# A gated MLP block: fifteen of sixteen token tiles transposed by DMA as f16 parts, in place of f32 transposes on TensorE

## The chip, the cores and the metric

The kernel runs on one core of one Trainium2 chip, in one launch. The metric is the device time of that launch in microseconds (us), which is better when it is lower. Times of a kernel are given as the median of several executions; one more execution is recorded by the hardware profiler, and its rows are what this document quotes. TensorE is the matrix engine, VectorE, ScalarE and POOL are the vector engines, and SP only issues DMAs. In the rows they are called PE (PEld is TensorE's loading of weights), DVE, ACT, POOL and SP (SPq is the queue of DMAs that SP issues).

## The reference

One block works on 2048 tokens of width 576. A state space convolution comes first; its output x goes through a layer norm with learned scale and shift (from the condition c), then through a gated MLP whose gate mixes tokens:

```python
h = _layernorm(x, axis=-1) * (1 + cb) + sb
z = _gelu(jnp.einsum("bsd,df->bsf", h, w_in))        # 576 -> 4608
z1 = z[..., :Fh]                                     # Fh = 2304
z2 = _layernorm(z[..., Fh:], axis=-1)
g = jnp.einsum("ts,bsf->btf", w_sp, z2) + b_sp[None, :, None]
x = x + gb * jnp.einsum("bsf,fd->bsd", z1 * g, w_out)
```

The products are wanted to nearly f32 accuracy. The kernel gets this from f16 matmuls: each f32 operand is split into a high part hi = f16(v) and a low part lo = f16(v - hi), and hi·hi, hi·lo and lo·hi are added up in PSUM.

## The kernel before

The program has three stages. The convolution runs to about 443 us. Then phase_a, the z2 stage, makes h and the second half of z for all tokens, and prepares operands for later. From about 693 us phase_b makes z1, the token mixing g and the output; it takes more than half of the time, and the change does not touch it.

phase_a works on 16 token tiles of 128 rows. For tile b, x1_load(b) reads the 128x576 rows; ln2_stats(b), roots and ln2_rows(b) make the normalised rows n (tile n2, f32, 128x640: the last 64 columns are there twice, through a tensor_copy) on VectorE. turn(b) transposes n on TensorE in five 128x128 pieces against an identity, into the PSUM tile pt. turn_hi(b) on ScalarE and turn_lo(b) on VectorE read pt and write the f16 parts into nt: nine slabs of 128 tokens, four of high parts, four of low parts, and a ninth that has the last 64 columns as high parts on partitions 0 to 63 and as low parts on 64 to 127. turn_lo also stores nt to DRAM (n2_d) through POOL's queue, for phase_b.

z2_mm(b, h) multiplies nt with the weights wz for column block h: five blocks, four of 512 columns and one of 256, 14 matmuls each, so 70 a tile. z2_gelu(b, h) takes each block out of PSUM (six banks, tile pz) through gelu into z, on ScalarE. There are two z buffers. z2_stats collects statistics on VectorE (bsz), roots(b) turns them into scale and shift (nm), z2_diff and z2_norm normalise z in place, and z2_store(b) writes it to DRAM (z2_d) through POOL's queue in two DMAs.

All of phase_a goes through an object that keeps every engine's instructions in the order in which the program calls them, SP's DMAs as well. In the main loop (line 1243) the iteration of tile b holds, in this order: DMAs due (LD); z2_mm(b,0); due squares (A0); gelu (b,0); statistics and roots of tile b-1 and of the rows of tile b+2; z2_norm(b-1); ln2_rows(b+2); x1_load(b+4); z2_mm(b,1); turn(b+1); gelu (b,1); z2_store(b-1); z2_stats of the first columns; turn_hi(b+1); turn_lo(b+1); z2_mm(b,2); gelu (b,2); further due work (A1); z2_mm(b,3), gelu, more statistics; ln2_stats(b+3); due work (V1); z2_mm(b,4), gelu.

The due work belongs to later stages. side_load, side_sum, side_hi and side_lo split the first half of w_in (tiles wst, wso). wsp_load and out_load read pieces of w_sp and w_out (tile wsst, two buffers, two pieces a tile) in A1 of one iteration, and norm_sp and norm_out square and sum them on ScalarE in A0 of the next, ahead of its gelu (b,0). block_load, wsp_sums, wsp_hi and wsp_lo (tile xz) prepare w_sp from tile 8 on.

The first iteration is special, since the weights wz are still being made there. For the blocks q = 3 and 4, start_sum(q) squares the raw weights on ScalarE (its junk output goes to wz), win_scale(5 + q) forms a total over partitions on TensorE (two small matmuls pz<-acc,ones) and a power-of-two scale on VectorE, start_hi(q) writes the high parts on ScalarE and start_lo(q) the low parts on VectorE. They stand in iteration 0: start_sum(3) and win_scale(8) ahead of gelu (0,0), start_hi(3) and start_lo(3) behind it, then roots, ln2_rows(2), z2_mm(0,1), gelu (0,1), start_sum(4), win_scale(9), start_hi(4) and start_lo(4). Ahead of the loop (line 1230) tile 0 is transposed and the rows of tile 1 are made.

Of the kernel before, what the change touches and what calls it, by code (L numbers as in the profile page):

```python
# [9 lines left out]
F32 = mybir.dt.float32  # L10
F16 = mybir.dt.float16
BF = mybir.dt.bfloat16
I32 = mybir.dt.int32
AF = mybir.ActivationFunctionType
ALU = mybir.AluOpType
# [3 lines left out]
D = 576  # L19
# [742 lines left out]
class Mlp:  # L762
# [342 lines left out]
    def ln2_rows(self, b):  # L1105

        V = self.nc.vector
        x, m, r = self.xts.pop(b), self.mvx.pop(b)[:, 0, 0:1], self.rx.pop(b)
        n = self.ns[b] = self.ap.tile([128, 640], F32, name="n2")
        V.scalar_tensor_tensor(n[:, :D], x, m, self.mrow[:, 1], op0=ALU.subtract, op1=ALU.mult)  # L1110
        V.scalar_tensor_tensor(n[:, :D], n[:, :D], r, self.mrow[:, 0], op0=ALU.mult, op1=ALU.add)
        V.tensor_copy(n[:, D:], n[:, 512:D])

    def turn(self, b):

# [53 lines left out]
            self.nc.gpsimd.dma_start(self.z2_d[:, b // 4, :, 2 * (b % 2) + h, b % 4 // 2].rearrange("f p c -> p f c"), z[:, h])  # L1169

    def phase_a(self):
        self.prods, self.z1s, self.n2, self.bsp, self.gbs, self.wfs = {}, {}, {}, {}, {}, {}
        ap = self.ap = self.pool(self.c2, "ap", 2)
        cpa = ExitStack()
        self.pa = self.pool(cpa, "pa", 6, space=PSUM)
        self.ps1 = lambda: self.pa.tile([128, 512], F32, name="pz")
        self.zp = self.pool(self.c2, "zp", 2)
        self.wp = self.pool(self.ctx, "wp", 7, side="right")

        self.fp = self.pool(self.ctx, "fp", 1, side="right")  # L1180
        self.wso = ap.tile([128, 4, 10, 128], F16, name="wso", bufs=1)
        self.nc, plain = self.tied, self.nc
        self.nc.vector.memset(self.wso[64:, :, 9], 0.0)

        LD, PE, A0, A1, V0, V1 = range(6)
        sides = [[[] for _ in range(6)] for _ in range(17)]

        def side(b, k, fn, *a):
            sides[b][k].append((fn, a))

        def do(b, k):
            for fn, a in sides[b][k]:
                fn(*a)

        for q in range(5):
            side(2 * q, LD, self.side_load, q)
            side(2 * q + 1, A0, self.side_sum, q)
            side(2 * q + 1, PE, self.win_scale, q)
            side(2 * q + 1, A1, self.side_hi, q)
            side(2 * q + 1, V1, self.side_last, q)  # L1200
            side(2 * q + 1, V1, self.side_lo, q, 0)
            side(2 * q + 2, V0, self.side_lo, q, 1)
        for h in range(2):
            side(1, LD, self.bsp_load, ap, h)
            side(2, A0, self.norm_bsp, h)
        for i in range(8):
            side(2 + i // 2, A1, self.wsp_load, 0, i, ap)
            side(3 + i // 2, A0, self.norm_sp, 0, i)
        for i in range(12):
            side(6 + i // 2, A1, self.out_load, ap, i)  # L1210
            side(7 + i // 2, A0, self.norm_out, i)
        for i in range(6):
            side(12 + i // 2, A1, self.wsp_load, 1, i, ap)
            side(13 + i // 2, A0, self.norm_sp, 1, i)
        side(13, V1, self.sums_out)
        side(14, PE, self.scales_out)
        side(6, V1, self.sums_sp, 0)
        side(7, PE, self.scales_sp, 0)
        side(11, PE, self.scales_gate, 0)
        for i in range(7):  # L1220
            side(9 + i, V0, self.wsp_sums, i)
            side(9 + i, A1, self.wsp_hi, 0, i)
            side(9 + i, V1, self.wsp_lo, 0, i)
            side(8 + i, V1, self.block_load, 0, i)
        side(13, LD, self.z1_rows, 0)
        side(13, LD, self.bias_load, 0)
        for f in (0, 9, 1):
            side(13, LD, self.z1_load, 0, f)

        for b in range(2):  # L1230
            if b == 1:
                self.ln2_stats(1)
                self.roots(x=1)
                self.ln2_rows(1)
            if b == 0:
                self.turn(0)
                self.turn_hi(0)
                self.start_lo(2)
                self.start_load(4)
                self.x1_load(4)  # L1240
                self.turn_lo(0)
        self.ln2_stats(2)
        for b in range(16):
            do(b, LD)
            self.z2_mm(b, 0)
            do(b, A0)
            if b == 0:
                self.start_sum(3)
                self.win_scale(8)
            self.z2_gelu(b, 0)  # L1250
            if b == 0:
                self.start_hi(3)
                self.start_lo(3)
            if b > 0:
                self.z2_stats(b - 1, 5)
            self.roots(b - 1 if b > 0 else None, b + 2 if b + 2 < 16 else None)
            if b > 0:
                if b % 2:
                    self.z2_diff(b - 1)
                self.z2_norm(b - 1)  # L1260
            if b + 2 < 16:
                self.ln2_rows(b + 2)
            if 4 < b + 4 < 16:
                self.x1_load(b + 4)
            do(b, PE)
            self.z2_mm(b, 1)
            if b + 1 < 16:
                self.turn(b + 1)
            self.z2_gelu(b, 1)
            if b > 0:  # L1270
                self.z2_store(b - 1)
            if b == 0:
                self.start_sum(4)
                self.win_scale(9)
                self.start_hi(4)
            do(b, V0)
            self.z2_stats(b, 0, 1)
            if b + 1 < 16:
                self.turn_hi(b + 1)
            if b == 0:  # L1280
                self.start_lo(4)
            if b + 1 < 16:
                self.turn_lo(b + 1)
            self.z2_mm(b, 2)
            self.z2_gelu(b, 2)
            do(b, A1)
            self.z2_mm(b, 3)
            self.z2_stats(b, 2, 3)
            self.z2_gelu(b, 3)
            if b + 3 < 16:  # L1290
                self.ln2_stats(b + 3)
            do(b, V1)
            self.z2_stats(b, 4)
            self.z2_mm(b, 4)
            self.z2_gelu(b, 4)
        cpa.close()
        self.z2_stats(15, 5)
        self.roots(15)
        self.z2_norm(15)
        self.z2_store(15)  # L1300
        self.nc = plain
        self.c2.close()
# [315 lines left out]
```

## Time and profile before

| | us |
|---|---|
| median of 3 executions (1796.09 to 1799.17) | 1798.02 |
| the profiled execution | 1798.62 |
| its span, first to last instruction | 1796.9 |
| TensorE busy, whole span | 1695.7 |
| VectorE busy | 1128.8 |
| ScalarE busy | 785.6 |
| z2 stage, from the first transposes to the last z2 product | about 250 |

The page of the profile gives totals over the whole span. Other views cut it: busy time by stage, the timeline (every instruction with its start, its duration and, in brackets, the idle time before it and what ended it), the groups of instructions of one shape, the list of waits, and the DMA issues with the time from issue to landing. Nearly all work of phase_a goes through one helper line (L132), so its rows are told apart by the tiles that they write and read: pt<-ident,n is a transpose on TensorE, pz<-wz,nt a z2 product, z<-pz,sc a gelu, z<-z,nm,r a normalisation, wsst<-wsst a square for a norm.

### The profile page before, as it was taken

What the parts mean: (1) busy time and instruction counts of PE and PEld (TensorE: products, weight loads), DVE (VectorE), ACT (ScalarE), POOL (GpSimd) and SP (SyncE); (2) the same over time, 40 slices, a digit from 0 to 9 for tenths busy, and PEclk for the clock granted to TensorE, in tenths of its full rate; (3) what the DMA queues carried; (4) which work ended last, traced back from release to release, by engine and by line L of the source; (5) the groups of instructions that cost most, each with busy time, mean ns of one, the idle gap of its engine ahead of it and who ended that gap; (6) DMA issues with size and microseconds to landing.
All of it is one profiled execution on the core that took longest, in us unless ns stands there. A gap on an engine that the chain in (4) does not pass through costs nothing.

```text
span 1796.9 us, 34078 instructions
## 1 busy us (share of the span) xinstructions
PE 1695.7 (94%) x14202; PEld 1197.6 (67%) x14202; DVE 1128.8 (63%) x2253; ACT 785.6 (44%) x1021; POOL 224.0 (12%) x350
## 2 busy tenths in 40 slices
PE   4687999996899999999999999999999999999999
PEld 1344555565455545877787777877778777887787
DVE  6987999857888997999784444474222265222322
ACT  4658999844476666555441322241111132011110
POOL 1321232342122211000000000000000000000000
PEclk8788999998899999999999999999999999999999
DMA  8457445779588788877564675562655472555520
GB/s 274 139 196 243 139 119 163 195 207 314 169 266 261 241 259 246 301 277 257 206 216 148 240 250 206 212 250 92 227 192 197 173 264 69 176 181 175 199 83 27
DMA packets 153034, 361.57 MB, mean 201 GB/s; under 512 B 24832, under 2 KB 68224, under 8 KB 150960
## 3 DMA queue, kind: packets, MB, share of 16 engines
q1 hardware_dynamic: 110272, 167.30, 29.4%
q0 software_dynamic: 33120, 153.95, 25.8%
q10 hardware_dynamic: 9488, 38.16, 5.3%
q8 instruction: 111, 1.82, 0.4%
q14 instruction: 43, 0.35, 0.1%
HBM read 256.86 MB, written 93.05 MB: 195 GB/s over the span
## 4 chain that ended last, share of the span: by engine, by line
PE 51%; DVE 16%; DMA 7%; issue 4%; ACT 4%; SPq 0%; POOL 0%; ACTq 0%; DVEq 0%; POOLq 0%
PE ps L1324 9%; PE ps L1359 8%; PE ps L1361 8%; PE ps L1360 8%; PE pz L132 3%; PE ps L1408 3%; PE ps L1409 3%; PE ps L1410 3%; DMA raw<-in_w_spT 2%; DVE zset L1066 2%; DVE gt L1373 2%; DMA z_d<-z 2%; ACT z L132 1%; DVE bsz L132 1%; PE pk L132 1%
## 5 line engine op out<-in xcount | busy, mean ns | idle before, releaser
L1359 PE MATMUL ps<-wsp,zset 128*128 128x256 f16 x2016 | 549.5, 273 | 2.8 <-DVE gt L1373 2.6
L1361 PE MATMUL ps<-wsp,zset 128*128 128x256 f16 x2016 | 549.5, 273 | 0.2 <-DVE zset L1066 0.2
L1360 PE MATMUL ps<-wsp,zset 128*128 128x256 f16 x2016 | 549.5, 273 | 0.0
L132 PE MATMUL pz<-wz,nt 128*128 128x512 f16 (+1 forms) x1120 | 227.2, 363 | 9.0 <-ACT nt L132 5.5
L1373 DVE SCALAR_TENSOR_TENSOR gt<-ps,sc,bsp 128x512 f32<-128x512 f32 x36 | 27.0, 749 | 316.1 <-PE ps L1361 316.1
L1324 PE MATMUL ps<-n2q,wf 128*128 128x512 f16 x1008 | 223.3, 379 | 0.6 <-DMA wf<-win_d 0.6
L1359 PEld LDWEIGHTS <-zset 128*128 128x128 f16 x2016 | 197.5, 98 | 29.7 <-DVE gt L1373 3.2
L1360 PEld LDWEIGHTS <-zset 128*128 128x128 f16 x2016 | 197.2, 98 | 26.1
L1361 PEld LDWEIGHTS <-zset 128*128 128x128 f16 x2016 | 197.3, 98 | 23.3 <-DVE zset L1066 0.5
L132 PEld LDWEIGHTS <-nt 128*128 128x128 f16 x1120 | 110.2, 100 | 117.4 <-ACT nt L132 7.2
L1324 PEld LDWEIGHTS <-wf 128*128 128x128 f16 x1008 | 98.6, 98 | 112.6 <-DMA wf<-win_d 1.1
L1336 POOL DMA_DIRECT2D zset<-set_d x96 | 51.1, 532 | 969.3 <-PE ps L1361 939.3
L1329 ACT ACTIVATE z<-ps,sc 128x512 f32<-128x512 f32 x56 | 37.8, 681 | 280.5 <-PE ps L1324 278.0
L1409 PE MATMUL ps<-wout,z 128*128 128x288 f16 x448 | 128.1, 286 | 0.0
L1408 PE MATMUL ps<-wout,z 128*128 128x288 f16 x448 | 128.1, 286 | 0.0
L1410 PE MATMUL ps<-wout,z 128*128 128x288 f16 x448 | 128.1, 286 | 0.0
L1373 DVE SCALAR_TENSOR_TENSOR gt<-ps,sc,gt 128x512 f32<-128x512 f32 (+1 forms) x180 | 121.9, 694 | 5.8 <-DVE gt L1373 0.5
L1066 DVE TENSOR_TENSOR zset<-raw,zset 128x1024 f16<-128x1024 f32 x48 | 58.6, 1220 | 74.7 <-ACT zset L1065 74.7
L1065 ACT ACTIVATE zset<-raw 128x1024 f16<-128x1024 f32 x48 | 50.3, 1051 | 97.5 <-PE ps L1361 70.1
L132 ACT ACTIVATE z<-pz,sc 128x512 f32<-128x512 f32 (+1 forms) x80 | 49.6, 646 | 56.8 <-DMA z_d<-z 44.4
L1418 DVE TENSOR_TENSOR ot<-ot,ps 128x288 f32<-128x288 f32 x32 | 14.2, 452 | 82.7 <-ACT ot L1417 82.7
L369 PE MATMUL ps<-ln_x,r1t 128*128 128x288 f32 x128 | 43.6, 499 | 19.0 <-issue 12.6
(311 smaller groups left out, 2827.5 us busy)
## 6 DMA issues: line engine op xcount, KB each, us to landing
zset<-set_d POOLq DMA_DIRECT2D x96, 896.0 KB, 4.9
set_d<-zset ACTq DMA_DIRECT2D x36, 896.0 KB, 5.8
raw<-z_d SPq DMA_DIRECT2D x48, 512.0 KB, 4.6
wf<-win_d SPq DMA_DIRECT2D x72, 320.0 KB, 3.4
raw<-in_w_spT SPq DMA_DIRECT2D x43, 512.0 KB, 6.0
z_d<-z POOLq DMA_DIRECT2D x32, 576.0 KB, 7.8
u_d<-st1o POOLq DMA_DIRECT2D x16, 576.0 KB, 4.5
u<-u_d SPq DMA_DIRECT2D x36, 256.0 KB, 4.8
```

What stands on the lines that cost most here:

```text
L132: return self.tc.keep_in_program_order(f(*a, **k))
L1065: nc.scalar.activation(o[:, k, 0], t, AF.Copy)
L1066: nc.vector.tensor_tensor(o[:, k, 1], t, o[:, k, 0], op=ALU.subtract)
L1324: nc.tensor.matmul(pm.rearrange("p (t c) -> p t c", t=4), w[:, kw], self.n2[q][:, :, kn], start=i == 0, stop=i == len(Z1) - 1)
L1336: self.nc.gpsimd.dma_start(o, self.set_d[n // 4, n % 4])
L1359: T.matmul(pm, z[:, a, 0, c], w[:, b, 0], start=i + half == 0, stop=False, skip_group_check=True)
L1360: T.matmul(pm, z[:, a, 0, c], w[:, b, 1], start=False, stop=False, skip_group_check=True)
L1361: T.matmul(pm, z[:, a, 1, c], w[:, b, 0], start=False, stop=i == 7, skip_group_check=True)
L1373: V.scalar_tensor_tensor(dst, pm, inv, to, op0=ALU.mult, op1=ALU.add)
L1408: T.matmul(pl, p[:, 1, ts], w[:, 0, hs], start=st, stop=sp)
L1409: T.matmul(pa, p[:, 0, ts], w[:, 0, hs], start=st, stop=False)
L1410: T.matmul(pa, p[:, 0, ts], w[:, 1, hs], start=False, stop=sp)
```

## The change

For tiles 1 to 15 the rows are split as they lie, tokens on partitions, and the f16 result is transposed by a DMA on SP's queue. Tile 0 keeps turn, turn_hi and turn_lo. Four new functions stand for the three:

```diff
-        n = self.ns[b] = self.ap.tile([128, 640], F32, name="n2")
+        n = self.ns[b] = self.ap.tile([128, 640], F32, name="n2", bufs=1)
...
-        V.tensor_copy(n[:, D:], n[:, 512:D])
+        if b == 0:
+            V.tensor_copy(n[:, D:], n[:, 512:D])
+
+    def rows_hi(self, b):
+        A, n = self.nc.scalar, self.ns[b]
+        o = self.nrs[b] = self.ap.tile([128, 9, 128], F16, name="nr", bufs=1)
+        A.activation(o[:, 0:4], n[:, :512].rearrange("p (k c) -> p k c", k=4), AF.Copy)
+        A.activation(o[:, 8, :64], n[:, 512:D], AF.Copy)
+
+    def rows_lo(self, b):
+        V, n, o = self.nc.vector, self.ns.pop(b), self.nrs[b]
+        V.tensor_tensor(o[:, 4:8], n[:, :512].rearrange("p (k c) -> p k c", k=4), o[:, 0:4], op=ALU.subtract)
+        V.tensor_tensor(o[:, 8, 64:], n[:, 512:D], o[:, 8, :64], op=ALU.subtract)
+
+    def rows_turn(self, b):
+        nt = self.nts[b] = self.ap.tile([128, 9, 128], F16, name="nt", bufs=3)
+        self.nc.sync.dma_start_transpose(nt, self.nrs.pop(b).rearrange("p k c -> p (k c)"))
+
+    def rows_store(self, b):
+        self.nc.gpsimd.dma_start(self.n2_d[b // 4, :, b % 4], self.nts[b])
```

Their places in phase_a: tile 1 is split and transposed ahead of the loop, and iteration b splits and transposes tile b+2, one tile earlier than turn did, while it stores the nt of tile b+1.

```diff
@@ ahead of the loop, b == 1
                 self.ln2_rows(1)
+                self.rows_hi(1)
+                self.rows_lo(1)
+                self.rows_turn(1)
@@ in the loop
             self.z2_mm(b, 1)
-            if b + 1 < 16:
-                self.turn(b + 1)
+            if b + 2 < 16:
+                self.rows_hi(b + 2)
             self.z2_gelu(b, 1)
...
             self.z2_stats(b, 0, 1)
-            if b + 1 < 16:
-                self.turn_hi(b + 1)
             if b == 0:
                 self.start_lo(4)
+            if b + 2 < 16:
+                self.rows_lo(b + 2)
+                self.rows_turn(b + 2)
             if b + 1 < 16:
-                self.turn_lo(b + 1)
+                self.rows_store(b + 1)
             self.z2_mm(b, 2)
```

n2 has one buffer instead of two, and nr, the split rows, has one.

More of the change, by code (lines that the diff above doesn't have):

```diff
@@ L1171, in phase_a @@
     def phase_a(self):
+        self.nrs = {}
         self.prods, self.z1s, self.n2, self.bsp, self.gbs, self.wfs = {}, {}, {}, {}, {}, {}
```

## The prediction

> **What bounds the kernel now.** First I read the busy time by stage, cut at the borders of the z2 loop (first transposes 443 us, last z2 product 693 us).
>
> ```profile
> core 0: us, PE busy (x) PEld busy (x) DVE busy (x) ACT busy (x) POOL busy (x), PEclk, DMA share, GB/s
> 444.00:474.00 30.00, 22.43 (x93) 10.56 (x93) 26.49 (x79) 13.28 (x16) 3.36 (x5) 0.83 0.59 188
> 507.00:693.00 186.00, 178.87 (x947) 92.93 (x946) 162.99 (x497) 121.40 (x181) 39.18 (x51) 1.00 0.82 255
> ```
>
> Two regimes. From 507 us on TensorE is 96% busy, VectorE 88%, the DMA engines 82%: TensorE leads, the others close behind. In the first 30 us TensorE is a quarter idle at a granted clock of 0.83, and VectorE (26.5 of 30 us) leads. Next the timeline of one steady tile, TensorE:
>
> ```profile
> 565.31 0.71 PE L132 MATMUL pt<-ident,n 128*128 128x128 f32 x5
> 565.86 13.78 PE L132 MATMUL pz<-wz,nt 128*128 128x512 f16 x70
> 579.48 0.71 PE L132 MATMUL pt<-ident,n 128*128 128x128 f32 x5
> ```
>
> Five transposes take 565.86 - 565.31 = 0.55 us, and the 70 products of a tile 579.48 - 565.86 = 13.62 us. So all that TensorE can save is 15 x 0.55 = 8.3 us. The timeline of ScalarE gives what a tile really takes, from the first gelu of tile 3 to that of tile 15:
>
> ```profile
> 507.27 0.69 ACT L132 ACTIVATE z<-pz,sc 128x512 f32<-128x512 f32 x1 [2.32 <-DMA z_d<-z]
> 689.33 0.69 ACT L132 ACTIVATE z<-pz,sc 128x512 f32<-128x512 f32 x1 [4.55 <-DMA z_d<-z]
> ```
>
> 182.06 / 12 = 15.17 us a tile. Both rows end a wait for an older store of z (two z buffers); the list of waits between 460 and 680 us has 39.8 us of these. So TensorE has 1 us of stalls a tile over its 14.17, and a second ring (gelu, normalise, store, buffer free) runs near the same length.
>
> ```profile
> ACT z L132 <- DMA z_d<-z: 39.8, 11, 7.8
> ```
>
> **The change: the start of the loop.** In the loop every engine keeps the order of the program. rows_hi(1) now stands on ScalarE ahead of start_sum(3), and rows_hi(2) ahead of gelu (0,1) and start_sum(4). Both need rows that VectorE makes late. Before, in rows (ScalarE, VectorE, TensorE):
>
> ```profile
> 447.26 2.34 ACT L132 ACTIVATE wz<-wst 128x2560 f16<-128x2560 f32 x1 [2.40 <-DMA wst<-in_w_in]
> 449.50 0.19 ACT L132 ACTIVATION_READ_ACCUMULATOR wz<-wst 128x1 f32 x1
> 456.49 2.00 ACT L132 ACTIVATE wz<-wst,sc 128x2048 f16<-128x2048 f32 x1 [5.37 <-DVE sc L132]
> 458.40 0.67 ACT L132 ACTIVATE z<-pz,sc 128x512 f32<-128x512 f32 x1
> 458.97 1.26 ACT L132 ACTIVATE wz<-wst 128x1280 f16<-128x1280 f32 x1
> ...
> 453.26 0.82 DVE L132 SCALAR_TENSOR_TENSOR n<-n,rx,mrow 128x576 f32<-128x576 f32 x1
> 455.30 0.16 DVE L132 COPY sc<-pz 128x1 f32<-128x1 f32 x1
> 465.20 0.82 DVE L132 SCALAR_TENSOR_TENSOR n<-n,rx,mrow 128x576 f32<-128x576 f32 x1
> ...
> 450.19 0.42 PE L132 MATMUL pz<-acc,ones 128*128 128x1 f32 x2
> 460.37 0.58 PE L132 MATMUL pz<-acc,ones 128*128 128x1 f32 x2 [4.90 <-ACT wz L132]
> 460.82 13.66 PE L132 MATMUL pz<-wz,nt 128*128 128x512 f16 x56
> ```
>
> Step by step, after the change:
> - Row 1 is ready when its second operation ends, 453.26 + 0.82 = 454.1. rows_hi(1) takes 0.8 (below): 454.9. start_sum(3) with its readout takes 449.69 - 447.26 = 2.43: 457.3. From readout to the total in PSUM 450.61 - 449.69 = 0.92: 458.25. From VectorE's copy to start_hi(3) 456.49 - 455.30 = 1.19: start_hi(3) begins at 459.45 instead of 456.49, 3.0 late.
> - Between start_hi(3) and the end of row 2 stand start_lo(3), the roots and the row itself on VectorE: 466.02 - 456.49 = 9.53. Row 2 is ready at 469.0; rows_hi(2) until 469.8; gelu (0,1) 0.57; start_sum(4) with readout 1.35: 471.8. Only then can TensorE form the total of win_scale(9), which stood at 460.37: 11.4 us late. Everything behind it on TensorE, the 56 products from 460.82 on, is late by as much; VectorE and ScalarE by 7, then by TensorE's 11.
> - Back come two turns (1.1 us) and VectorE's idle pieces. Cost of the start: **+10 us** (7 if ScalarE's shift sets it, 12 at most). It rests on order and rows of before alone, with no unknown price in it.
>
> **The steady tiles.** Each removes five transposes (0.55), a VectorE copy of 64 columns, and splits read from PSUM; it adds the same splits from SBUF. Their prices from rows of SBUF sources:
>
> ```profile
> L132 ACT ACTIVATE wso<-wst,sc 128x512 f16<-128x512 f32 x18 | 11.6, 727 | 0.0
> L132 DVE SCALAR_TENSOR_TENSOR wso<-wst,sc,wso 128x512 f16<-128x512 f32 x18 | 12.6, 740 | 0.0
> L132 DVE TENSOR_TENSOR nt<-pt,nt 128x512 f16<-128x512 f32 x14 | 9.6, 687 | 0.5
> ```
>
> 0.73 and 0.74 us for the 512 columns, against 0.69 from PSUM on VectorE; with 64 columns more 0.8 and 0.9: even, worth nothing either way. Single buffers for n2 and nr: n2 is read and rewritten by VectorE in order; nr is refilled some 11 us after its transpose is issued (the transpose follows the place of VectorE's 572.77 below, the next rows_hi ScalarE's 569.14 a tile later, 584.3), so that costs nothing unless the transpose takes longer. The store of nt on POOL finds its data a tile old.
>
> What matters is SP's queue. rows_turn(b+2) waits on SP for rows_lo(b+2), and behind it stand the two loads for the norms (out_load, wsp_load) of tile b+1, whose squares stand on ScalarE ahead of gelu (b+1,0). Before, those loads went right behind x1_load:
>
> ```profile
> 567.78 0.91 SPq L132 DMA_DIRECT2D wsst<-in_w_out  x2
> ...
> 565.68 0.69 ACT L132 ACTIVATE z<-pz,sc 128x512 f32<-128x512 f32 x1 [2.10 <-DMA z_d<-z]
> 566.74 1.35 ACT L132 ACTIVATE z<-z,nm,r 128x1152 f32<-128x1152 f32 x1 [0.38 <-DVE z L132]
> 569.14 0.67 ACT L132 ACTIVATE z<-pz,sc 128x512 f32<-128x512 f32 x1
> 571.84 1.01 DVE L132 BATCH_NORM_STATS2 bsz<-z 128x6 f32<-128x384 f32 x2
> 572.77 1.00 DVE L132 TENSOR_TENSOR nt<-pt,nt 128x512 f16<-128x512 f32 x2
> 574.30 0.94 ACT L132 ACTIVATE wsst<-wsst 128x864 f32<-128x864 f32 x1
> 576.02 0.21 ACT L132 ACTIVATION_READ_ACCUMULATOR wsst<-wsst 128x1 f32 x1
> ```
>
> They were issued at 567.78 and used at 574.30, 6.5 us later. Now rows_lo (where 572.77 stood) comes first, so they leave some 6 us later and ScalarE waits. This closes a ring, once per tile: transpose issued (X), loads land (L after issue), squares 576.23 - 574.30 = 1.93, gelu 0.57, normalising 569.14 - 566.74 = 2.40, rows_hi 0.8, gelu (b+1,1) 0.57, statistics 572.77 - 571.84 = 0.93, rows_lo 0.9, and an estimated 0.4 for the first issue and the hops: **X + L + 8.5 us** a tile, for twelve tiles (transposes 4 to 15).
>
> ```profile
> wsst<-in_w_spT SPq DMA_DIRECT2D x14, 512.0 KB, 6.3
> wsst<-in_w_out SPq DMA_DIRECT2D x12, 432.0 KB, 4.5
> n_d<-nt POOLq DMA_DIRECT2D x16, 288.0 KB, 7.5
> ...
> 567.40 0.33 SPq L132 DMA_DIRECT2D x1t<-x_d  x1
> 667.57 2.68 SPq L132 DMA_DIRECT2D wsst<-in_w_spT  x2
> ```
>
> Six tiles have L = 6.3, six 4.5: mean 5.4. No row shows a transposing DMA. For X the rows of SP bound it: 0.33 (a plain issue) to 1.34 (the longest here, 2.68 / 2); I take the upper, 1.3, since it must be made of more pieces than a plain one. Its bytes (288 KB) are bounded below by nothing, hidden in L, and above by the store of the same 288 KB, 7.5 to landing under this load. I take them as hidden. The ring is then 1.3 + 5.4 + 8.5 = **15.2 us**, the 15.17 of before: 12 x 0 = no change. The 0.55 of TensorE is saved and not used. The store ring may shorten, since the loads no longer go out just ahead of it, but it is then not the longest.
>
> The Trainium skill (Advanced Engine Details and Errata, X-Bar Transpose (TRN2)) says that transposing DMAs on this chip are as fast as ordinary ones; that would leave the bytes hidden, as I take them. It speaks against the change elsewhere (VectorE: DVE Perf Modes, The three transpose paths): 1309 ns for one 128x128 tile by DMA against 390 ns on TensorE. Here the trace has 0.11 us on TensorE for one of the five, so the page's comparison is even kinder to DMA than this kernel; nine tiles at 1309 ns would be an estimated 11.8 us on the queue, a ring of some 25 us and a time near 1930. No run here shows it yet.
>
> **Sum.** Start +10, steady 0: the profiled execution took 1798.62 us (span 1796.9) and would take 1808.6. The median of the runs shown is 1798.02, 0.6 lower; carried over, **1808 us**. Later stages are only shifted: they start from the last z2 store.
>
> **The rivals.**
> 1. Faster: the loads land early (X = 0.33, L = 4.5 for all, because the stores no longer meet them: ring 13.3), and TensorE's floor of 13.62 + 0.1 is what is left. 12 x (13.7 - 15.17) = -17.6, with the start -7.6: 1790. For it: TensorE is 96% busy; against: VectorE has 162.99 / 186 x 15.17 = 13.3 us of work per tile and a gap at each rows_hi, and the store ring.
> 2. No change: the ring settles at 14.4 (VectorE's 13.3 and a gap of 1): -9 and +10, 1799.
> 3. Slower, far: the loads must wait for the transposed bytes ahead of them on SP's queue. From a price of about 3 us on it decides over everything else. At the 7.5 us of the 288 KB store, with 2 us more for the loads, L = 9.5: ring 19.3, 12 x 4.1 = +49 and +10: 1857. The single nr would then wait too. With half the extra ring, 1832. The Trainium skill's 1309 ns a tile (VectorE: DVE Perf Modes, The three transpose paths, above) points this way; no row here has it.
> 4. The change doesn't do what it says: the start's order doesn't hold ScalarE. Then 1798 with the ring at 15.2; the rows of the start are all in program order, so little speaks for it.
>
> **Chances.** Forecast (ring 14.8 to 17, 1802 to 1830) 0.50; rival 3 beyond 1830 0.17; rival 2 and 4 0.14; rival 1 0.19. A measurement of this kernel tells about 0.2%, 3.6 us, from no change: faster 0.19, same 0.14, slower 0.67. The range takes in rival 1's end and half of rival 3: 1790 to 1842.
>
> **What would show it.** Right: ScalarE's first wz square at about 455 instead of 447, the second near 470, TensorE's second total near 472; SP waiting for VectorE's nr; ScalarE's wsst squares waiting for their DMA in tiles 3 to 14, in place of z for z_d. Wrong: no wait at wsst (the ring isn't closed), wsst landing later than 8 us (rival 3), or TensorE back to back at 13.6 us a tile (rival 1). A stall at nr on ScalarE would show that the transpose lasts over 11 us.

## The result and the profile after

| | before | after |
|---|---|---|
| median of 4 executions, us | 1797.58 (1796.09 to 1799.17) | 1855.61 (1848.13 to 1858.62) |
| the profiled execution | 1798.62 | 1856.82 |
| its span | 1796.9 | 1855.0 |

The ratio is 1.0316 (95% interval 1.0284 to 1.0349): the change costs 58 us. First the page of the kernel after: the busy times and the DMA packets by size.

```profile
PE 1701.0 (92%) x14127; PEld 1193.5 (64%) x14127; DVE 1123.2 (61%) x2238; ACT 785.1 (42%) x1021; POOL 223.6 (12%) x350
...
DMA packets 170794, 366.00 MB, mean 197 GB/s; under 512 B 42592, under 2 KB 85984, under 8 KB 168720
```

No engine has notably more work: VectorE has less than before (1128.8), ScalarE the same (785.6), TensorE 5 us more, though it has 75 instructions fewer (14202 before). The time was lost in waiting. Busy time by stage of the kernel after, in the windows of before, the second one drawn out to the end of the longer stage (columns: window, us, then busy us and instructions of each engine, granted clock, DMA share, GB/s):

```profile
core 0: us, PE busy (x) PEld busy (x) DVE busy (x) ACT busy (x) POOL busy (x), PEclk, DMA share, GB/s
444.00:474.00 30.00, 12.45 (x40) 4.98 (x41) 21.43 (x67) 9.81 (x14) 2.07 (x4) 0.72 0.41 122
507.00:745.00 238.00, 193.74 (x930) 93.91 (x929) 162.52 (x503) 124.59 (x184) 38.86 (x50) 0.91 0.82 223
```

In the steady tiles TensorE fell from 96% busy (178.87 of 186) to 81% (193.74 of 238), and its granted clock from 1.00 to 0.91; at the start it has 12.45 us of work where it had 22.43. What ScalarE waits for there, in the list of waits between 460 and 680 us (us in total, times, longest):

```profile
ACT wsst L132 <- DMA wsst<-in_w_out: 45.6, 6, 10.0
...
ACT wsst L132 <- DMA wsst<-in_w_spT: 36.6, 8, 9.7
...
ACT z L132 <- DMA z_d<-z: 2.0, 1, 2.0
```

The 39.8 us of waits for the z store have gone, and 82.2 us of waits for the loads of the norms have come. To place the 58 us, here are the first gelus of tiles 2, 14 and 15 on the timeline, and the first products of phase_b, after:

```profile
498.45 0.69 ACT L132 ACTIVATE z<-pz,sc 128x512 f32<-128x512 f32 x1 [1.96 <-DMA z_d<-z]
728.45 0.67 ACT L132 ACTIVATE z<-pz,sc 128x512 f32<-128x512 f32 x1
742.53 0.69 ACT L132 ACTIVATE z<-pz,sc 128x512 f32<-128x512 f32 x1 [5.37 <-DMA z_d<-z]
744.37 1.89 PE L1348 MATMUL ps<-n2q,wf 128*128 128x512 f16 x8
```

And before (tile 15 stands at 689.33 in the prediction):

```profile
490.42 0.69 ACT L132 ACTIVATE z<-pz,sc 128x512 f32<-128x512 f32 x1 [1.33 <-DMA z_d<-z]
675.39 0.69 ACT L132 ACTIVATE z<-pz,sc 128x512 f32<-128x512 f32 x1 [6.91 <-PE pz L132]
693.02 2.32 PE L1324 MATMUL ps<-n2q,wf 128*128 128x512 f16 x10
```

- Up to tile 2: 498.45 - 490.42 = **8.0** us late.
- Tiles 2 to 14, the twelve that have the loads of the norms behind a transpose: 230.00 against 184.97 us, **+45.0**, or 19.17 a tile against 15.41.
- Tile 15 (no transpose is left): 14.08 against 13.94 us. To the first product of phase_b: 1.84 against 3.69.
- Behind it: 1855.0 - 744.37 = 1110.6 against 1796.9 - 693.02 = 1103.9, **+6.7**. TensorE waits 9.8 us there in the first 256 us where it waited 5.0, mostly for VectorE's gt and zset. Two kernels of the experiments below have 1108.5 (the kernel before, normalise first) and 1107.9 us (both moves) there, so much of the 6.7 may be what this stage varies by.

Sum: 8.0 + 45.0 + 0.1 - 1.8 + 6.7 = 58.0.

Now the ring itself. SP's queue in two steady tiles of the kernel after (start, time on the queue), then ScalarE's first square behind the first loads:

```profile
585.74 1.99 SPq L132 DMA_TRANSPOSE nt<-nr  x1
588.16 2.41 SPq L132 DMA_DIRECT2D wsst<-in_w_out  x2
...
604.96 2.37 SPq L132 DMA_TRANSPOSE nt<-nr  x1
607.37 2.91 SPq L132 DMA_DIRECT2D wsst<-in_w_out  x2
...
597.17 0.92 ACT L132 ACTIVATE wsst<-wsst 128x864 f32<-128x864 f32 x1 [9.05 <-DMA wsst<-in_w_out]
```

From transpose to loads 2.4 us, from loads to squares 597.17 - 588.16 = 9.0, from squares to the next transpose 7.8: 19.2 us. ScalarE idles 9.05 us of it for data alone. The prices of the two unknown terms, from the DMA issues (KB, median us from issue to landing) and from the view of the tile nr (issue min/median/max in ns):

```profile
wsst<-in_w_spT SPq DMA_DIRECT2D x14, 512.0 KB, 8.2
wsst<-in_w_out SPq DMA_DIRECT2D x12, 432.0 KB, 8.4
...
L132 SPq DMA_TRANSPOSE nt<-nr x15: 1285/2202/3161, 454.6 to 715.9; - x15
...
DMA to landing us min/median/max: 3.2/8.7/10.3
```

X is 2.2 and L is 8.3: X + L + 8.5 = 19.0, against 19.17 measured. The loads land 2 to 4 us later after their issue than before (6.3 and 4.5). Two things changed for them at once. On SP's queue the transpose stands ahead; and on POOL's queue the z store (1152 KB), which used to leave behind them, now leaves ahead. The timeline of before,

```profile
596.89 0.85 SPq L132 DMA_DIRECT2D wsst<-in_w_out  x2
...
601.20 2.02 POOL L132 DMA_DIRECT2D z_d<-z  x2 [11.82 <-ACT z L132]
```

and of after, where the loads of the same kind follow at 607.37:

```profile
602.56 2.03 POOL L132 DMA_DIRECT2D z_d<-z  x2 [15.53 <-ACT z L132]
```

Over the tiles of the ring the store's issue stands 3.7 to 5.5 us ahead of the loads'.

The start, ScalarE and TensorE of the kernel after:

```profile
453.11 0.78 ACT L132 ACTIVATE nr<-n 128x512 f16<-128x512 f32 x2 [8.72 <-DVE n L132]
453.79 2.32 ACT L132 ACTIVATE wz<-wst 128x2560 f16<-128x2560 f32 x1
...
467.64 0.78 ACT L132 ACTIVATE nr<-n 128x512 f16<-128x512 f32 x2 [7.56 <-DVE n L132]
...
468.89 1.26 ACT L132 ACTIVATE wz<-wst 128x1280 f16<-128x1280 f32 x1
...
470.29 0.59 PE L132 MATMUL pz<-acc,ones 128*128 128x1 f32 x2 [8.66 <-ACT wz L132]
```

ScalarE waits twice for rows of VectorE (8.72 and 7.56 us), and the weights' sums stand behind: TensorE's second total is at 470.29 instead of 460.37, 9.9 late. (The first transposes come at 442.50 and before at 443.29; counted from there it is 10.7 late.)

### The profile page after: what moved, and what is told of

It reads as the page before. It is cut to its first block, busy times and chain, and to the rows that moved or that the text cites. A ratio compares the mean times of both kernels' runs of the same rounds, so it can differ in the third digit from the quotient of the medians.

```text
span 1855.0 us, 33912 instructions
## 1 busy us (share of the span) xinstructions
PE 1701.0 (92%) x14127; PEld 1193.5 (64%) x14127; DVE 1123.2 (61%) x2238; ACT 785.1 (42%) x1021; POOL 223.6 (12%) x350
## 2 busy tenths in 40 slices
DMA packets 170794, 366.00 MB, mean 197 GB/s; under 512 B 42592, under 2 KB 85984, under 8 KB 168720
## 3 DMA queue, kind: packets, MB, share of 16 engines
q1 hardware_dynamic: 128032, 171.72, 30.1%
## 4 chain that ended last, share of the span: by engine, by line
PE 48%; DMA 12%; DVE 9%; ACT 7%; issue 6%; SPq 1%; ACTq 0%; POOL 0%; DVEq 0%; POOLq 0%
PE ps L1383 9%; PE ps L1384 8%; PE ps L1385 8%; PE ps L1348 8%; ACT z L132 3%; DMA wsst<-in_w_spT 2%; DMA wsst<-in_w_out 2%; PE ps L1432 2%; PE pz L132 2%; PE ps L1434 2%; PE ps L1433 2%; DVE zset L1066 2%; DMA raw<-in_w_spT 2%; DVE gt L1397 2%; SPq L132 1%
## 5 line engine op out<-in xcount | busy, mean ns | idle before, releaser
L132 PE MATMUL pz<-wz,nt 128*128 128x512 f16 (+1 forms) x1120 | 235.4, 373 | 11.5 <-DMA nt<-nr 4.9
L132 DVE BATCH_NORM_STATS2 bsz<-z 128x6 f32<-128x384 f32 x96 | 50.2, 549 | 49.7 <-ACT z L132 49.7
L132 ACT ACTIVATE wsst<-wsst 128x1024 f32<-128x1024 f32 (+1 forms) x28 | 28.0, 1000 | 107.5 <-DMA wsst<-in_w_spT 53.6
```

Of the source, the lines that this page charges most:

```text
L132: return self.tc.keep_in_program_order(f(*a, **k))
```

## The experiments

The first theory after the result: two causes, both orders of queues. On SP the loads of the norms stand behind the transpose, so they leave late and then have to wait for its bytes; on ScalarE the splits of rows 1 and 2 stand ahead of the weights. Rivals: the transposing itself is slow or fills the DMA engines, or something else in the steady tiles (the single nr, the splits) sets the time. The last four experiments test the z store, which had moved ahead of the loads too; they overturned the half of the theory that blames the transpose's bytes. Times are medians, each ratio is against the kernel before on the same chip.

**Loads first.** The loads of the norms get a slot of their own (SL) behind x1_load(b+4), ahead of the transpose on SP.

```diff
-            side(2 + i // 2, A1, self.wsp_load, 0, i, ap)
+            side(2 + i // 2, SL, self.wsp_load, 0, i, ap)
...
-            side(6 + i // 2, A1, self.out_load, ap, i)
+            side(6 + i // 2, SL, self.out_load, ap, i)
...
                 self.x1_load(b + 4)
+            do(b, SL)
```

> The changed kernel, with the two norm loads of a tile issued on SP behind x1_load and ahead of rows_turn, where the kernel before had them. Ring theory (the loads are late because they stand behind the transpose on SP): the waits of ScalarE's wsst squares, 107 us in all, go to under 15, a tile falls from 18.9 to 15.2 us or less, about 1806 us (the start's 8 to 10 us stay). Crowding theory (the transposes' small packets slow every DMA): the loads still need some 8 us to land and the z stores come later, a tile stays above 17 us, 1830 or more.

1805.43 us, ratio 1.0044 (1.0026 to 1.0062): 50 us of the 58 come back. The list of waits, 460 to 680 us:

```profile
ACT wsst L132 <- DMA wsst<-in_w_spT: 7.5, 3, 4.4
...
ACT wsst L132 <- DMA wsst<-in_w_out: 1.5, 1, 1.5
```

The waits at wsst fall from 82.2 to 9.0 us, and those for the z store return (28.4 us). The transposes are no cheaper (3.2 us on the queue, 9.2 to landing): with nothing urgent behind them that costs little. The ring of the loads sets the time; why they land late this run can't tell, since it moves them ahead of the transpose and ahead of the z store alike.

**Start order.** The splits of row 1 go behind start_lo(3), rows_hi(2) behind start_hi(4); the loads stay as in the change.

```diff
-                self.rows_hi(1)
-                self.rows_lo(1)
-                self.rows_turn(1)
...
                 self.start_lo(3)
+                self.rows_hi(1)
+                self.rows_lo(1)
+                self.rows_turn(1)
...
-            if b + 2 < 16:
+            if 0 < b and b + 2 < 16:
                 self.rows_hi(b + 2)
...
                 self.start_hi(4)
+                self.rows_hi(2)
```

> The changed kernel, with rows_hi(1), rows_lo(1) and rows_turn(1) moved behind start_lo(3), and rows_hi(2) behind start_hi(4), so that ScalarE squares the weights at once again. Start theory: TensorE's second total goes from 470.3 back to about 461 us and the time falls by 8 to 10 us, to about 1846. If the ring sets the time wherever it starts, or the later tiles take the gain up: 1855.

1843.19 us, ratio 1.0259 (1.0225 to 1.0292), 12.4 us under the change. TensorE's second total comes 17.3 us after the first transposes (440.99 to 458.30), where it came 27.8 after them in the change and 17.1 before.

**Both moves** together.

> Both moves together. If the two costs are all there is and they add up: 1793 to 1799, and below 1797 only if a tile gets under 15.2 us. With TensorE's floor of 13.7 us a tile: 1780 to 1785. Crowding theory: 1820 or more.

1797.04 us, ratio 1.0005 (0.9981 to 1.0029): no difference from before. Against loads first alone the start order is worth 1805.43 - 1797.04 = 8.4 us, so it is worth 8 to 12, and the ring about 46 to 50. Nothing else of the 58 us is left. But nothing of TensorE's 0.55 us a tile shows either. This kernel's list of waits, 460 to 680 us:

```profile
ACT z L132 <- DMA z_d<-z: 33.1, 13, 5.0
```

and its windows:

```profile
507.00:680.00 173.00, 163.61 (x831) 81.58 (x830) 148.06 (x451) 113.69 (x169) 38.06 (x50) 0.98 1.01 275
```

As before, gelu waits for the z store; TensorE is 95% busy; the DMA engines' share in these windows went from 0.81 before to 1.01.

**A plain copy.** The change, with an ordinary DMA of the same 288 KB from nr to nt at the same place. The rows are not transposed, so the products are of other numbers.

```diff
-        self.nc.sync.dma_start_transpose(nt, self.nrs.pop(b).rearrange("p k c -> p (k c)"))
+        self.nc.sync.dma_start(nt, self.nrs.pop(b))
```

> The changed kernel in its order, with an ordinary DMA copy of nr into nt in the place of the transposing DMA (the rows are then not transposed, so nt holds other values). If a transposing DMA is dear in itself: SP's issue falls from 2.2 to about 0.4 us, the loads land in 5 to 6 us instead of 8.2, ring 14 to 15 us, 1800 to 1808. If only the order counts, whatever the DMA: the loads still take some 8 us, ring 17, 1830 or more.

1839.15 us, ratio 1.0240 (1.0206 to 1.0274). Its DMA issues:

```profile
wsst<-in_w_spT SPq DMA_DIRECT2D x14, 512.0 KB, 9.7
wsst<-in_w_out SPq DMA_DIRECT2D x12, 432.0 KB, 8.9
nt<-nr SPq DMA_DIRECT2D x15, 288.0 KB, 7.8
```

The loads land as late with an ordinary 288 KB transfer ahead of them as with the transposing one (9.7 and 8.9 against 8.2 and 8.4), and 42 of the 58 us stay. So it is not the transposing as such. The copy saves some 16 us, 13 of them in the tiles of the ring (first gelus of tiles 2 and 14 at 495.36 and 712.11: 18.06 us a tile against 19.17). It holds the queue 0.5 us instead of 2.2, but the loads land 1.0 us later after their issue; these two alone would make 12 x 0.7 = 8 us, and what makes the rest is not shown.

**Loads from ScalarE's queue.** The change, with the loads of the norms issued by ScalarE at the same place of the program.

```diff
-        return self.nc.sync.dma_start(t, self.I["w_out"].rearrange("(p a) b -> p (a b)", p=128)[:, 864 * i:864 * i + 864])
+        return self.nc.scalar.dma_start(t, self.I["w_out"].rearrange("(p a) b -> p (a b)", p=128)[:, 864 * i:864 * i + 864])
```

(wsp_load in the same way.)

> The changed kernel, with the two norm loads of a tile issued from ScalarE's queue at the same place of the program (behind gelu (b,2)), so that they stand behind no transpose but still leave after the z store. Queue theory (the loads take 8.2 us because the transposed bytes are ahead of them on SP's queue): they land in some 5.5 us, a tile is 15.2 us, about 1806. Bytes theory (they take 8.2 us because the 1.1 MB z store went out just ahead of them and all DMAs share the engines): they still land in 8 us; squares 1.9, gelu 0.6, normalising 2.4, rows_hi 0.8, two gelus 1.2, issue 0.9 and 8.2 make a ring of 16.4 us, about 1820.

1815.19 us, ratio 1.0091 (1.0067 to 1.0116), 40 us under the change and between the two forecasts. Its DMA issues:

```profile
wsst<-in_w_spT ACTq DMA_DIRECT2D x14, 512.0 KB, 5.7
wsst<-in_w_out ACTq DMA_DIRECT2D x12, 432.0 KB, 4.7
```

The loads land in 5.7 and 4.7 us, what they took before the change. That looked like proof for the queue, but the queues' timeline takes it back: here the loads left with the z store (595.48 and 595.55 us in one tile) and 3 us ahead of the transpose (598.51), as ScalarE doesn't wait for the split rows where SP does. Both causes were taken away again. The z store lands later (9.3 against 6.9 us in the change) and its waits are back (33.2 us between 460 and 680), which eats part of the gain.

**Both moves, plain copy** (not transposed either): is it the transposing traffic that keeps both moves from gaining?

> The kernel with both moves (loads first, start in the old order) and an ordinary copy of nr into nt in place of the transposing DMA (rows not transposed, so other values). If the transposes' bytes on nearly full DMA engines (busy share 1.01) take what TensorE saves: the share falls to 0.85 to 0.9 and a tile to 14.2 us, 1783 to 1788. If the ring over the two z buffers is what is left, whatever the transposes cost: a tile stays at 15 us, 1793 to 1799.

1794.48 us, ratio 0.9982 (0.9967 to 0.9998), beside 1.0005 for both moves on another chip. The DMA share falls from 1.01 to 0.89, the time by some 3 us, within both intervals' reach. The waits of gelu for the z store are left in it (38.9 us between 460 and 680). So the transposes' traffic alone isn't what keeps the 8.3 us; some 3 of them it may.

**The z store split**, to shorten that ring: the second half of z is issued from ScalarE's queue right behind its normalisation, the first stays on POOL's; with both moves, and in the kernel before.

```diff
+        self.z2_half(A, b, 1)
+
+    def z2_half(self, Q, b, h):
+        z = self.zs[b].rearrange("p (h f c) -> p h f c", h=2, c=128)
+        Q.dma_start(self.z2_d[:, b // 4, :, 2 * (b % 2) + h, b % 4 // 2].rearrange("f p c -> p f c"), z[:, h])
...
+        self.z2_half(self.nc.gpsimd, b, 0)
+        self.zs.pop(b)
```

> The kernel with both moves, and the second half of each z store issued from ScalarE's queue right behind the normalisation, instead of as POOL's second DMA, which ends 2 us after it. If the ring over the two z buffers sets the tile: some 0.8 to 1 us less a tile, 1783 to 1788. If the DMA engines are simply full: no change, 1794 to 1799.

> The kernel before the change with the same split of the z store alone. If the ring over the z buffers holds there too: its tile falls from 15.2 to at most TensorE's 14.2 us, 1785 to 1789. If TensorE alone holds it: 1796 to 1798.

1804.92 us (1.0037, 1.0020 to 1.0054) and 1803.64 us (1.0036, 1.0017 to 1.0056): both slower by 0.4%, which neither theory forecast.

With both moves the halves land 8.7 (ScalarE's queue) and 9.0 us (POOL's) after their issue, later than the 7.8 us of both moves alone, and gelu still waits 30.0 us for them (30.1 in the kernel before). This says nothing on what the ring is worth.

**Half a z store.** Only the first half of each z tile is stored (the second is left out; phase_b reads the stored half twice, in two loads of half the size); with both moves, and in the kernel before.

```diff
...
-        for h in range(2):
+        for h in range(1):
             self.nc.gpsimd.dma_start(self.z2_d[:, b // 4, :, 2 * (b % 2) + h, b % 4 // 2].rearrange("f p c -> p f c"), z[:, h])
```

> The kernel with both moves, and only the first half of each z tile stored (576 KB instead of 1152; the later stage reads that half twice, in two loads of 256 KB in place of one of 512). If the ring over the two z buffers is what kept the tile at 15.1 us though TensorE needs 13.6: the waits of gelu for the z store (38 us) go to under 10 and a tile falls to 13.7 to 14.2 us, the first z1 product about 12 to 17 us earlier than with both moves (near 670 us). If something else holds it (VectorE, or DMA engines full of the transposes): still 14.8 or more.

> The kernel before the change with the same half store. If the z ring binds here too: a tile falls from 15.2 to TensorE's 14.2 us with its transposes. The difference to the kernel with both moves is then what the transposes by DMA are worth once TensorE is the bound: 12 x 0.55 = 7 us at most in the stage. If no gain is left between the two: under 2 us.

1787.82 us (0.9940, 0.9919 to 0.9961) and 1795.12 us (0.9988, 0.9971 to 1.0006). Busy time by stage, with both moves:

```profile
507.00:680.00 173.00, 171.04 (x881) 86.29 (x879) 157.20 (x480) 118.80 (x173) 25.86 (x37) 0.99 0.90 251
```

and before:

```profile
507.00:680.00 173.00, 171.55 (x910) 89.75 (x909) 158.52 (x482) 116.83 (x172) 25.62 (x38) 1.00 0.71 229
```

Now TensorE is 99% busy in both: it sets the pace. Their first gelus of tiles 3 and 15, with both moves:

```profile
500.34 0.69 ACT L132 ACTIVATE z<-pz,sc 128x512 f32<-128x512 f32 x1 [0.74 <-DMA z_d<-z]
666.35 0.69 ACT L132 ACTIVATE z<-pz,sc 128x512 f32<-128x512 f32 x1 [0.52 <-PE pz L132]
```

and before:

```profile
500.00 0.69 ACT L132 ACTIVATE z<-pz,sc 128x512 f32<-128x512 f32 x1
672.38 0.72 ACT L132 ACTIVATE z<-pz,sc 128x512 f32<-128x512 f32 x1
```

166.01 / 12 = 13.83 us a tile against 172.38 / 12 = 14.37. The difference is 0.54, the price of five transposes, and the whole time differs by 7.3 us. So the saving is there, and it appears once half of the z store is away: the store hides it in the kernel as it is. Half a store takes away bytes on the DMA engines as well as waits for a z buffer (4.8 and 7.9 us are left of those), so this pair alone doesn't say which of the two it is.

Against the kernels with the whole store the first product of phase_b comes 9.1 us earlier with both moves (676.69 against 685.76; 12 to 17 were forecast). In the kernel before it comes 6.7 us earlier, counted from TensorE's second total (226.0 us behind it against 232.7), but the whole time shows little of it: behind that product the profiled execution takes 1109.2 us against 1103.9.

**Normalise first.** The ring in complete kernels: z2_norm(b-1) moves ahead of gelu (b,0), so that a store leaves before ScalarE waits for an older one; with both moves, and in the kernel before.

```diff
-            self.z2_gelu(b, 0)
-            if b == 0:
+                self.z2_gelu(0, 0)
                 self.start_hi(3)
...
                 self.z2_norm(b - 1)
+                self.z2_gelu(b, 0)
```

> The kernel with both moves, and on ScalarE the normalisation of tile b-1 ahead of gelu (b,0) instead of behind it, nothing left out. Store ring theory: the normalisation no longer stands behind the gelu that waits for the older store, so a store leaves earlier and the ring runs over two tiles (from gelu (b,0) to (b,4) 11, gelu, statistics and roots 4.6, normalising 2.4, issue 2.3, landing 7.9: 28 us for two tiles); a tile falls from 15.1 to 14.1 us, 1783 to 1788. If the DMA engines or VectorE hold it: 1793 or more.

> The kernel before the change with the same move of the normalisation alone. Store ring theory: a tile falls from 15.2 to TensorE's 14.2 us, 1787 to 1791, some 3 to 7 us above the kernel with both moves and this one. If TensorE alone held the kernel before: no change.

With both moves 1800.18 us (1.0006, 0.9991 to 1.0021), no gain; in the kernel before 1793.06 us (0.9968, 0.9952 to 0.9984), short of the forecast, but the one complete kernel here that beats both. Waits of the second, 460 to 680 us:

```profile
ACT z L132 <- DVE nm L132: 33.3, 7, 7.1
ACT z L132 <- DVE z L132: 23.3, 7, 5.7
```

The waits for the z store are gone (1.6 us left), and ScalarE waits for VectorE's statistics and differences instead. The first has the same waits (31.7 and 24.6 us), a DMA share of 1.02 where the second has 0.83, and TensorE at 160.45 of 173 us where the second has 170.09 (the profiled execution of the first, 1807.00 us, is the longest of its twelve). Whether the fuller DMA engines or the order on VectorE holds the first back was not separated. So in the kernel before, the ring is shown to cost some 5 us; that it alone keeps both moves from gaining is not shown. A third z buffer, the direct way to open the ring, wasn't tried: there is no room for it beside the kernel's other tiles.

**Behind the store, not behind the transpose.** What makes the loads land late, the transfer ahead of them in SP's queue or the z store on POOL's? Two kernels keep the late place of the loads, but put a transfer of 64 bytes that waits for the split rows where the transpose stood; the transpose follows behind the loads. The second is the kernel before, where nothing is transposed by DMA and the 64 bytes wait for turn_lo.

```diff
+    def gate(self, s):
+        self.nc.sync.dma_start(self.ap.tile([1, 32], F16, name="gate"), s)
...
                 self.rows_lo(b + 2)
+                self.gate(self.nrs[b + 2][0:1, 8, 96:])
+            do(b, SL)
+            if b + 2 < 16:
                 self.rows_turn(b + 2)
```

> The change, but on SP a transfer of 64 bytes waits for the split rows in the transpose's place, the loads of the norms follow it, and the transpose goes behind them. So the loads leave as late as in the change (behind the z store and the wait), but not behind 288 KB on their queue. If they land late because they stand behind the transposing transfer in SP's queue: L falls from 8.3 to 5 to 6 us, the ring to about 0.5 + 5.5 + 8.5 = 14.5, below the z store's ring, and the time to 1805 to 1812. If they land late because the z store left 2 to 5 us ahead of them: L stays at about 8, the ring is about 17, the time 1825 to 1835, with waits at wsst as the longest.

> The kernel before, with nothing transposed by DMA, but the loads of the norms wait on SP behind a transfer of 64 bytes that waits for turn_lo's last result. If the queue's 288 KB make the loads late: L stays at 4.5 to 6.3, and with a ring of about 14 to 15 the time is 1797 to 1805. If being behind the z store does: L is about 8, the ring about 17, the time 1815 to 1825, with ScalarE waiting for wsst.

Two kernels keep the transpose ahead and take the store away: one issues it from SP behind the loads, the other stores only the first half of each z tile (the second half is left out, as above).

```diff
-            self.nc.gpsimd.dma_start(self.z2_d[:, b // 4, :, 2 * (b % 2) + h, b % 4 // 2].rearrange("f p c -> p f c"), z[:, h])
+            self.nc.sync.dma_start(self.z2_d[:, b // 4, :, 2 * (b % 2) + h, b % 4 // 2].rearrange("f p c -> p f c"), z[:, h])
...
             self.z2_gelu(b, 1)
-            if b > 0:
-                self.z2_store(b - 1)
...
             do(b, A1)
+            if b > 0:
+                self.z2_store(b - 1)
```

> The change, with the z store issued by SP behind the loads of the norms instead of by POOL ahead of them. The transpose stays ahead of the loads. If the transfer ahead in the queue makes the loads late: L stays at about 8 and the ring at 19, 1850 or more. If the z store does: L falls to 5 to 6, the ring to about 16.2, and the time to 1815 to 1830, unless the later z store sets the time instead.

> The change, with the second half of each z tile not stored (phase_b reads the first half twice): half the bytes of the store that leaves ahead of the loads. If the transfer ahead in the queue makes the loads late: L stays at about 8 and the time at 1845 to 1855. If the z store does: L falls to 6 to 7 and the time to 1825 to 1838.

| | median us, of two executions | ratio (95%) |
|---|---|---|
| change, loads ahead of the transpose, behind the store | 1853.22 | 1.0300 (1.0225 to 1.0375) |
| before, loads behind the store | 1842.08 | 1.0238 (1.0191 to 1.0286) |
| change, store behind the loads | 1896.11 | 1.0539 (1.0477 to 1.0600) |
| change, half a store | 1818.21 | 1.0106 (1.0062 to 1.0149) |

The landing decides, not the totals, since two of these kernels have costs of their own. The DMA issues of the kernel before with the loads behind the store:

```profile
wsst<-in_w_spT SPq DMA_DIRECT2D x14, 512.0 KB, 10.4
...
wsst<-in_w_out SPq DMA_DIRECT2D x12, 432.0 KB, 9.2
```

and its z store and its loads in one tile:

```profile
570.74 2.03 POOL L132 DMA_DIRECT2D z_d<-z  x2 [11.89 <-ACT z L132]
...
573.42 1.15 SPq L132 DMA_DIRECT2D wsst<-in_w_out  x2
```

Of the change with the store behind the loads, with the tile nr's view:

```profile
wsst<-in_w_spT SPq DMA_DIRECT2D x14, 512.0 KB, 5.7
...
wsst<-in_w_out SPq DMA_DIRECT2D x12, 432.0 KB, 4.4
...
L132 SPq DMA_TRANSPOSE nt<-nr x15: 1248/1304/1441, 453.6 to 739.2; - x15
...
DMA to landing us min/median/max: 3.2/3.2/3.6
```

Of the change with half a store:

```profile
wsst<-in_w_spT SPq DMA_DIRECT2D x14, 512.0 KB, 5.1
...
wsst<-in_w_out SPq DMA_DIRECT2D x12, 432.0 KB, 4.4
```

Four readings agree. Without any transpose ahead, but behind the store, the loads land in 9 to 10 us (the first kernel of the four: 10.5 and 9.2). With the transpose right ahead, but no store or half of one, they land in 4.4 to 5.7. So the z store is what they wait for, though it left on another queue, and the transposed bytes ahead of them cost nothing that shows. With half a store the loads leave 4.0 to 5.8 us behind it, and it lands in 5.7 (median), so it is nearly done by then. POOL's other stores don't explain the difference: with the store behind the loads they, too, leave behind them (the transposed rows' at 597.57 us, the loads at 595.20), but with half a store they stay ahead, and the loads still land early.

X is of the same origin: without the store the transpose holds SP's queue for 1.3 us and lands in 3.2, with it 2.2 and 8.7. X and L also belong together. In the change the loads leave 3.7 to 5.5 us behind the store, in the kernel before with the loads behind the store 2.0 to 3.1, with the plain copy 2.3 to 3.3, and the nearer they leave, the longer they take: from the store's issue to the first square it is 12.8, 12.0 and 12.3 us (medians of the twelve tiles), with half a store 9.8. And the kernel before with nothing but the loads moved takes 1842.08 us, the time of the change with its start mended (1843.19): the ring's cost needs no transposing DMA at all.

None of the four totals fell into the range that the right theory had given. The first two are longer than 1825 to 1835 and 1815 to 1825, since L is not about 8 there but 9.9 and 9.8, the mean of the two kinds of load. In the first, moreover, the transposes come last and hold the queue 5.1 us in the median, and TensorE waits 29.9 us for nt between 460 and 680. In the third (1815 to 1830 forecast), gelu waits 60.9 us for the later z store, the exception that its forecast named. The fourth is shorter than 1825 to 1838, with an L of 4.8 in place of 6 to 7.

## Why the prediction was wrong

It gave 1808 us (1790 to 1842), slower; measured 1855.6, slower and outside the range.

- **The step that failed** is the term L: "Six tiles have L = 6.3, six 4.5: mean 5.4." These medians were read where the loads leave ahead of the z store, and the step before had just moved them some 6 us later, behind it. There L is 8.3 (8.2 and 8.4). The text even said that "the loads no longer go out just ahead of it", and drew from that only a gain for the store, not the loss for the loads. 12 x 2.9 = 35 of the 45 us that the tiles of the ring lost.
- **X**, taken at the upper of two rows, 1.3 us, happens to be what the transpose takes without the store (1.304), and it is 2.2 behind it: 12 x 0.9 = 11 us, from the same collision. The split between L and X is one of this order; the kernel before with the loads behind the store has no X of a transpose, a larger L (9.8) and the time of the change with its start mended.
- **Its bytes hidden in L**: right. With the store away the loads land as fast behind the transpose (5.7 and 4.4 us) as they did before the change (6.3 and 4.5).
- **The ring's formula held**: with the measured X and L it gives 19.0 us a tile, measured 19.17, so the remaining 8.5 was right, and so was the new wait, down to its tiles. SP's own list of waits, 460 to 680 us:

```profile
SPq L132 <- DVE nr L132: 114.1, 12, 11.8
```

- **Rival 3** came out at the right time (1857) by a wrong mechanism: it made the loads wait for the transposed bytes, with a price (9.5) near the true L. That the times agree is luck. Its sign, "wsst landing later than 8 us", could not tell the two apart. Nor did the second sign, a wait for the single nr, come: in the change ScalarE never waits for the transpose to free it.
- **The start** was right in mechanism and size: forecast 11.4 us late at TensorE's second total and +10 in the time; measured 9.9 late, 8.0 at tile 2, and 8.4 and 12.4 by the two pairs of runs.
- **Splits** from SBUF were taken as even: VectorE's total fell by 5.6 us, ScalarE's by 0.5. Right.
- **Rival 1** (TensorE's floor) needed early loads and a short store ring. Early loads alone (both moves) give 1797; only with half a store is the floor there, 13.83 us a tile beside its 13.7.
- **Later stages** "only shifted": 6.7 us longer in the profiled execution, much of which may be what that stage varies by.
- On the two rules of the Trainium skill: that transposing DMAs are as fast as ordinary ones (Advanced Engine Details and Errata, X-Bar Transpose (TRN2)) agrees in the time to landing, 8.7 us against 7.8 of the plain copy, but not on the issuing queue, 2.2 against 0.5. The 1309 ns for one 128x128 tile (VectorE: DVE Perf Modes, The three transpose paths) would make an estimated 11.8 us of nine; they landed in 3.2 with the store away, so as a price for each of nine f16 tiles in one transfer it doesn't hold here. The rule that bore on the failed step was left out: DMAs of all issuing engines run on the same 16 DMA engines and interleave (DMA: Bandwidth & Descriptors, Issuing engines are not separate DMA queues). The loads behind POOL's store, 9.2 and 10.4 us against 4.4 and 5.7 ahead of it, agree with it.

## What to carry to other kernels

The time that a load takes to land belongs to its place: when a change moves its issue, look on every queue for the large transfers that now leave just ahead of it, and take the price from rows with such a neighbour. A saving on the busiest engine can stay invisible while another ring has the same length; shorten that ring in an experiment (here half a store), and see whether the saving appears. When a rival's time comes true, test its mechanism all the same: undoing a move takes away everything that the move brought.

## What the runs showed of the hardware

- A transposing DMA of 288 KB held SP's queue 1.3 us with no z store ahead of it, 2.2 behind the z store, and 5.1 right behind the store and the loads (medians); the plain copy held it 0.5 even behind the store.
- It was made of small packets: 17,760 more in the change than before, 1184 for each of 15 (170794 - 153034), all of them under 512 B; the kernels with the plain copy have 144 for each. The DMA share rose from 0.89 (both moves, plain copy) to 1.01 with the same GB/s (276 and 275).
- Halves of the z store issued from ScalarE's queue made 16,128 packets more in all than both moves alone (186922 against 170794), and landed 1 us later than from POOL's alone.
- In the change the granted clock of TensorE was 0.91 over the steady tiles, where it was busy 81% of the time, and 0.72 in the first 30 us, where it was busy 42%; before, it was 1.00 at 96% and 0.83 at 75%.
